# Diagonal sums on VectorE and GpSimd, y from the state on row tiles, and a compact state, from unit 8 on

## The chip, the cores and the metric

The kernel runs on one core of a Trainium2 chip. The core has five engines with queues of their own: TensorE (PE in the profile, with its weight loads apart as PEld), VectorE (DVE), ScalarE (ACT), GpSimd (POOL) and SyncE (SP, which here issues DMAs only). The metric is the device time of one execution in microseconds (us). The kernel before takes 174.02 us, the median of three runs (173.86 to 175.29).

## The reference

The reference has two stages. The first is a linear recurrence for 4 batches and 8 heads over 768 steps, with 48 x 48 states. The second is a two-layer feed-forward stage with a squared ReLU on the 3072 rows that come out of it.

```python
for t in range(S):
    cur = np.einsum('bhd,bhe->bhde', u[None] * kt, vt)
    y[:, :, t] = np.einsum('bhd,bhde->bhe', rt, state + cur)
    state = w[None, :, :, None] * state + np.einsum('bhd,bhe->bhde', kt, vt)
...
x = y.transpose(0, 2, 1, 3).reshape(B * S, H * D)      # 3072 x 384
h = x @ w_in                                           # 384 -> 2048
out = np.maximum(h, 0.0) ** 2 @ w_out                  # 2048 -> 384
```

What matters here is that y of one step has three parts: what earlier steps of the same chunk give (q k^T with a mask, times v), what the state at the chunk's start gives, and the diagonal: the step's own v, weighted for each head by the sum over d of r * k * u. The last one is the "diagonal sum".

## The kernel before

The 768 steps are cut into 6 chunks of 128, and a chunk of one batch is a **unit**. There are 24 of them, numbered chunk by chunk, so units 4c to 4c + 3 are the batches of chunk c. The name of a step carries its unit: `mask:9:1` is the second mask of unit 9. A unit has the token (time step) on the partitions after its load; a transposed copy has head and d on them.

For each unit the steps are these (line numbers of the kernel before):

- `load` brings r, k and v; `scale` (L288, DVE) multiplies r and k by powers of w into the tile rkw, padded from 48 to 64 per head; `cast_v` (L292, ACT) makes v bf16 as vb; `turn` or `turn_dma` (L302) transposes rkw into rkT, through PE or through a DMA.
- `rk` (L320, DVE) multiplies the transposed r and k into the tile rk. `sums` (PE) makes the diagonal sums from rk with four matmuls against a matrix uwb of u / w (L348, 8 columns each), and four more for the chunk's state update (L353).
- `at` (L328, PE) makes q k^T on row tiles: a head pair's two heads lie on the upper and the lower 64 partitions, so eight matmuls of 64 rows write two banks. `ats` does two units at once, from unit 8 on. `mask` (L340, DVE) takes each bank through the strict triangle into the tile am.
- `y_mm` (PE) adds up y in one bank: eight matmuls of am with vb (L391), and from chunk 1 on four matmuls of rkT with the state stb (L397). stb has two heads side by side in a block-diagonal tile of 96 columns, zero off the blocks.
- `diag_v` (L362, DVE) multiplies vb by the diagonal sums into dv; `evict_y` (L406, DVE) adds dv and y into yb; `x_dma` or `x_turn` transposes it into xT for the second stage.
- `state_add` (L372) and `state_decay` (L376), both on DVE, bring the float32 state forward; `state_cast` (L382, ACT) writes stb in two copies, one for each half of the partitions.

In the second stage, `mm1` (L435, PE) makes four blocks of h for one unit in the first two chunks, and eight blocks for two units from unit 8 on; `relu` (L443, ACT) and `square` (L454 on DVE or L452 on ACT, by the last number of its name) make g; `mm2` (L461, PE) multiplies by w_out in quarters, `evict_o` (L468, ACT) copies out, and `store` (L495) is issued by POOL. `fill` (L233) is a matmul of 256 columns on a constant tile whose result nobody reads.

The order is written out: the string SCHEDULE lists all steps, each engine runs its own in that order, and the number behind an @ names the PSUM banks (eight in all) that a step takes. A step waits until its inputs are there and its bank or buffer is free, and everything behind it on its engine waits too.

## Time and profile before

| | |
|---|---|
| median of three runs | 174.02 us |
| the profiled execution, its own time | 173.05 us |
| its span on the core | 171.3 us |
| granted TensorE clock, mean | 0.99 |
| HBM read and written | 20.45 MB, 4.72 MB |

The span is the time from the first to the last instruction that the profile records; the execution's own time has 1.75 us more around it. Shares of busy time are of the span. In rows of groups the number before the bar counts the instructions, then come their busy time in us, the mean of one in ns, the idle time of the engine just before them, and what ended that. A timeline row starts with its start and duration in us. Durations of consecutive matmuls overlap, since they are pipelined; differences of starts tell what one costs in a stream. For DVE two neighbours overlap by some 0.08 us.

### The profile page before, as it was taken

To read this page: it belongs to the slowest core of one execution; us is meant where nothing else is said; L and a number is where in the kernel's file an instruction comes from. 1 tells how busy PE (TensorE), PEld (TensorE's weight loads), DVE (VectorE), ACT (ScalarE), POOL (GpSimd) and SP (SyncE) were. 2 spreads that over 40 slices of the span, in tenths; PEclk is the share of its full clock that TensorE was granted. 3 is DMA by queue.
4 is the path that set the end of the run, shared out by engine and by line. 5 is a ranking of instruction groups with operands and counts; after the bars stand their busy time and mean duration, and the time that the engine had idled before them with its cause. 6 is when DMAs were issued, how large, how long until landed. Compare 5 with 4: busy or idle time off the path is not lost.

```text
span 171.3 us, 4810 instructions
## 1 busy us (share of the span) xinstructions
PE 164.8 (96%) x1931; PEld 132.1 (77%) x1931; DVE 138.0 (81%) x298; ACT 120.8 (71%) x252; POOL 30.5 (18%) x62
## 2 busy tenths in 40 slices
PE   7949999999999999999999999999999999999993
PEld 3637998787887788697796896896898776999662
DVE  5457997879999999999989879988989797764800
ACT  4533669999699547788599599499359986295830
POOL 8989440000002200000300000303000030030010
PEclk9987999999999999999999999999999999999999
DMA  5999999989996999899999999999959994150014
GB/s 106 199 212 213 220 249 244 222 157 158 187 169 120 286 145 169 166 186 148 238 229 123 182 186 128 254 149 204 262 97 211 201 150 134 32 161 0 4 62 168
DMA packets 94784, 28.83 MB, mean 168 GB/s; under 512 B 90665, under 2 KB 92714, under 8 KB 94762
## 3 DMA queue, kind: packets, MB, share of 16 engines
q1 hardware_dynamic: 90512, 19.08, 71.8%
q0 software_dynamic: 4224, 9.44, 21.1%
q8 instruction: 15, 0.25, 0.6%
q14 instruction: 7, 0.06, 0.1%
q10 hardware_dynamic: 26, 0.00, 0.0%
HBM read 20.45 MB, written 4.72 MB: 147 GB/s over the span
## 4 chain that ended last, share of the span: by engine, by line
PE 87%; DVE 5%; DMA 4%; POOL 2%; issue 1%; POOLq 0%; DVEq 0%
PE bank L461 35%; PE bank L435 35%; DMA ldr<-in_r_dram 4%; PE bank L328 4%; PE bank L391 3%; PE bank L353 2%; PE bank L397 2%; PE bank L476 2%; PE bank L233 1%; PE bank L311 1%; PE bank L348 1%; DVE yb L406 1%; DVE am L340 1%; DVE st L370 1%; PE bank L421 1%
## 5 line engine op out<-in xcount | busy, mean ns | idle before, releaser
L443 ACT ACTIVATE gr<-bank 128x512 f32<-128x512 f32 x96 | 53.8, 603 | 27.8 <-PE bank L435 24.4
L435 PE MATMUL bank<-xT,w_in_q 128*128 128x128 bf16 (+1 forms) x768 | 70.6, 246 | 0.0
L461 PE MATMUL bank<-w_out_q,g 128*128 128x384 bf16 x368 | 67.6, 326 | 0.0
L435 PEld LDWEIGHTS <-w_in_q 128*128 128x128 bf16 x768 | 64.1, 113 | 2.4
L461 PEld LDWEIGHTS <-g 128*128 128x128 bf16 x368 | 34.0, 98 | 18.9 <-ACT g L452 0.5
L454 DVE TENSOR_TENSOR g<-gr 128x512 bf16<-128x512 f32 x50 | 33.0, 686 | 6.5 <-ACT gr L443 6.4
L495 POOL DMA_DIRECT2D out_dram<-osb x21 | 11.3, 543 | 130.3 <-ACT osb L468 119.6
L340 DVE TENSOR_TENSOR am<-bank,smask 128x512 bf16<-128x512 f32 x48 | 30.8, 684 | 3.5 <-PE bank L328 3.2
L452 ACT ACTIVATE g<-gr 128x512 bf16<-128x512 f32 x46 | 28.2, 633 | 0.5
L406 DVE TENSOR_TENSOR yb<-bank,dv 128x384 bf16<-128x384 f32 x24 | 13.3, 556 | 3.9 <-PE bank L391 1.2
L288 DVE TENSOR_TENSOR rkw<-ldr,wpos 128x384 bf16<-128x384 f32 x24 | 12.9, 552 | 3.8 <-ACT wpos L241 2.2
L382 ACT CAST stb<-st 64x192 bf16<-64x192 f32 x40 | 13.9, 348 | 2.2 <-DVE st L376 1.9
L362 DVE TENSOR_TENSOR dv<-vb,bank 128x384 f32<-128x384 bf16 x24 | 13.0, 549 | 2.9 <-PE bank L353 2.1
L288 DVE TENSOR_TENSOR rkw<-ldk,wneg 128x384 bf16<-128x384 f32 x24 | 13.1, 552 | 0.6 <-DMA ldk<-in_k_dram 0.5
L292 ACT CAST vb<-ldv 128x384 bf16<-128x384 f32 x24 | 12.2, 512 | 0.6 <-DMA ldv<-in_v_dram 0.4
L468 ACT COPY osb<-bank 128x384 f32<-128x384 f32 x23 | 10.6, 481 | 2.7 <-PE bank L461 2.7
L372 DVE TENSOR_TENSOR st<-bank,st 64x192 f32<-64x192 f32 x32 | 11.3, 352 | 1.3 <-PE bank L353 1.0
L320 DVE TENSOR_TENSOR rk<-rkT 128x512 bf16<-128x512 bf16 x24 | 10.1, 419 | 1.9 <-ACT rkT L315 1.4
L233 PE MATMUL bank<-warm 128*128 128x256 bf16 x53 | 10.0, 336 | 1.2 <-DVE warm L179 1.2
L315 ACT COPY rkT<-bank 128x512 bf16<-128x512 bf16 x12 | 6.6, 591 | 4.1 <-PE bank L311 4.0
L328 PEld LDWEIGHTS <-rkT 64*128 64x128 bf16 x192 | 5.6, 95 | 4.6 <-issue 4.4
L328 PE MATMUL bank<-rkT 64*128 64x128 bf16 x192 | 8.1, 220 | 0.8 <-ACT rkT L315 0.8
(58 smaller groups left out, 112.6 us busy)
## 6 DMA issues: line engine op xcount, KB each, us to landing
ldk<-in_k_dram SPq DMA_DIRECT2D x22, 192.0 KB, 4.3
out_dram<-osb POOLq DMA_DIRECT2D x21, 192.0 KB, 3.5
ldr<-in_r_dram SPq DMA_DIRECT2D x20, 192.0 KB, 4.3
ldv<-in_v_dram SPq DMA_DIRECT2D x19, 192.0 KB, 4.5
w_in_q<-in_moe_w_in_dram POOLq DMA_DIRECT2D x4, 384.0 KB, 9.6
w_out_q<-in_moe_w_out_dram POOLq DMA_DIRECT2D x4, 384.0 KB, 10.8
ldv<-in_v_dram POOLq DMA_DIRECT2D x5, 192.0 KB, 9.6
ldr<-in_r_dram POOLq DMA_DIRECT2D x4, 192.0 KB, 8.9
```

The costliest lines, as they stand in the source:

```text
L288: nc.vector.tensor_tensor(t["rkw"][:, x, :, :, :D], pair(src), pair(wx), ALU.mult)
L292: nc.scalar.copy(tiles[i]["vb"], tiles[i]["vt"])
L328: nc.tensor.matmul(out=t["at"][o][:, p, :], lhsT=t["rkT"][sl, 1, p, :], rhs=t["rkT"][sl, 0, p, :], start=True, stop=True,)
L340: nc.vector.tensor_tensor(am, t["at"][o], smask.unsqueeze(1).to_broadcast([C, HP, C]), ALU.mult)
L362: nc.vector.tensor_tensor(t["dv"], t["vb"], t["d"].unsqueeze(2).to_broadcast([C, H, D]), ALU.mult)
L382: nc.scalar.copy(stb[b][sl, :, o * D : (o + 1) * D], st32[b][sl])
L406: nc.vector.tensor_tensor(t["yb"], t["y"], t["dv"].rearrange("p h d -> p (h d)"), ALU.add)
L435: nc.tensor.matmul(out=t["h", s][:, a], lhsT=turned, rhs=chunks[c]["xT"][:, n, b : b + m, :], start=(n == 0), stop=(n == NK - 1),)
L443: nc.scalar.activation(t["gr", s], t["h", s], AF.Relu)
L452: nc.scalar.activation(g, x, AF.Square)
L454: nc.vector.tensor_tensor(g, x, x, ALU.mult)
L461: nc.tensor.matmul(out=t["o"], lhsT=chunks[units[i][0]]["g"][:, f, units[i][1], :], rhs=w_out_q[f // 4][:, f % 4, :], start=(f == 0), stop ...
```

## The change

From unit 8 on (chunk 2 and later) three things are done in another way, and the order of all steps is written anew:

- **Diagonal sums.** `rk` and the four L348 matmuls go. In token layout, `product` (DVE) multiplies scaled r and k of the 384 real columns into pr; `weigh` (POOL) multiplies by u / w, which two broadcast loads (`wide_load`) and one product (`wide_product`) put on all partitions once; two `fold` steps (POOL) add halves of each head, 48 to 24 to 12; `head_sums` (DVE) reduces the last 12. `diag_v` reads the sums from SBUF instead of PSUM.
- **y.** The state's part is made by eight matmuls of 64 rows and 48 columns a unit, right behind q k^T of both units inside `ats`, in two banks (even heads and odd heads) that hold both units. `ys` adds the mask's part of both units. `evict_y` reads two half tiles.
- **State.** The bf16 state stc keeps one head's 48 columns on each half of the partitions, with no zeros, so `state_cast` is one copy; this begins with the casts of unit 4, which unit 8 reads.

`ats` thus takes six banks where it took four. Of 96 squares, DVE has 30 where it had 50, and ACT 66 where it had 46. Of fills there are 34 where there were 53.

```diff
+    WIDE_FROM = 8
...
+    stc = [const.tile([128, HP, D], BF16, name=f"stc_{b}") for b in range(B)]
+    wide = [const.tile([128, H, D], F32, name=f"wide{x}") for x in range(2)]
...
+    def wide_load(x):
+        src = (w, u)[x].rearrange("h d -> (h d)").unsqueeze(0).to_broadcast([128, dm])
+        nc.sync.dma_start(out=wide[x].rearrange("p h d -> p (h d)"), in_=src)
+    def wide_product():
+        nc.gpsimd.tensor_tensor(wide[1], wide[1], wide[0], ALU.mult)
+    def product(i):
+        t = tiles[i]
+        t["pr"] = buffer("pr", [C, H, D], BF16)
+        nc.vector.tensor_tensor(pair(t["pr"]), t["rkw"][:, 0, :, :, :D], t["rkw"][:, 1, :, :, :D], ALU.mult)
+    def weigh(i):
+        t = tiles[i]
+        t["pw"] = buffer("pw", [C, H, D], F32)
+        nc.gpsimd.tensor_tensor(t["pw"], t["pr"], wide[1], ALU.mult)
+    def fold(i, n):
+        x = tiles[i]["pw"]
+        m = D >> (n + 1)
+        nc.gpsimd.tensor_tensor(x[:, :, :m], x[:, :, :m], x[:, :, m : 2 * m], ALU.add)
+    def head_sums(i):
+        t = tiles[i]
+        t["d"] = buffer("ds", [C, H], F32)
+        nc.vector.tensor_reduce(out=t["d"], in_=t["pw"][:, :, : D // 4], axis=mybir.AxisListType.X, op=ALU.add)
...
     def ats(i):
         at(i)
         at(i + 1)
+        for j in (i, i + 1):
+            y = halves(j)
+            for p in range(HP):
+                for o in range(2):
+                    sl = slice(o * 64, o * 64 + 64)
+                    nc.tensor.matmul(
+                        out=y[o][:, p, :], lhsT=tiles[j]["rkT"][sl, 0, p, :], rhs=stc[units[j][1]][sl, p, :],
+                        start=(j == i and p == 0), stop=False, skip_group_check=True,
+                    )
...
-        for p in range(HP):
+        for p in range(HP if i < WIDE_FROM else 0):
             nc.tensor.matmul(
                 out=t["d"], lhsT=t["rk"][:, p, :], rhs=uwb[:, p, :],
...
+        if i >= WIDE_FROM - B:
+            nc.scalar.copy(stc[b], st32[b])
+        for o in range(2 if i < WIDE_FROM - B else 0):
...
+    def ys(i):
+        for j in (i, i + 1):
+            t = tiles[j]
+            y = halves(j)
+            for p in range(HP):
+                for o in range(2):
+                    nc.tensor.matmul(
+                        out=y[o][:, p, :], lhsT=t[f"am{o}"][:, p, :], rhs=t["vb"][:, 2 * p + o, :],
+                        start=False, stop=j > i and p == HP - 1, skip_group_check=True,
+                    )
...
+        if i >= WIDE_FROM:
+            out_y = t["yb"].rearrange("c (a o d) -> c o a d", o=2, d=D)
+            dv = t["dv"].rearrange("c (a o) d -> c o a d", o=2)
+            for o, y in enumerate(halves(i)):
+                nc.vector.tensor_tensor(out_y[:, o], y, dv[:, o], ALU.add)
+            return
```

The schedule's first line, before and after:

```diff
-load:1:kt:SP fill:256@7 load:0:rt:SP 2*fill:256@7 load:0:kt:SP 2*fill:256@7 load:1:rt:POOL 2*fill:256@7 load:2:kt:SP
+load:0:rt:SP load:1:kt:SP load:0:kt:SP load:1:rt:POOL load:2:kt:SP columns:1 columns:0 load:2:rt:POOL spread_log@0
```

Three places show what moves. On PE before, `sums` of unit 16 has the four diagonal matmuls (rk, uwb) ahead of those for the state (vb, rkw):

```order
L348 LDWEIGHTS rk_2134
L348 MATMUL bank7_68<-uwb_145,rk_2134 128x8
L348 LDWEIGHTS rk_2134
L348 MATMUL bank7_68<-uwb_145,rk_2134 128x8
L348 LDWEIGHTS rk_2134
L348 MATMUL bank7_68<-uwb_145,rk_2134 128x8
L348 LDWEIGHTS rk_2134
L348 MATMUL bank7_68<-uwb_145,rk_2134 128x8
L353 LDWEIGHTS rkw4_121
L353 MATMUL bank7_68<-vb_2152,rkw4_121 128x96
```

On PE after, the end of q k^T of units 16 and 17 (L363) is followed by the state's part of y of unit 16 (L379), whose halves go to banks 3 and 7:

```order
L363 LDWEIGHTS rkT_2027
L363 MATMUL bank4_65<-rkT_2027 128x128
L363 LDWEIGHTS rkT_2027
L363 MATMUL bank2_63<-rkT_2027 128x128
L379 LDWEIGHTS rkT_2089
L379 MATMUL bank3_64<-stc_0_160,rkT_2089 128x48
L379 LDWEIGHTS rkT_2089
L379 MATMUL bank7_68<-stc_0_160,rkT_2089 128x48
L379 LDWEIGHTS rkT_2089
L379 MATMUL bank3_64<-stc_0_160,rkT_2089 128x48
```

The diagonal matmuls are gone from PE, and the state's part of y has moved ahead of the masks, onto the row tiles.

On DVE before, around the masks of units 16 and 17 (am), stand the two rk products and the decays of the state (st32):

```order
L320 TENSOR_TENSOR rk_2134<-rkT_1964 128x512
L340 TENSOR_TENSOR am1_2160<-bank4_65,smask_140 128x512
L376 TENSOR_TENSOR st32_2_149<-st32_2_149,wend_c_159 128x192
L320 TENSOR_TENSOR rk_2170<-rkT_1995 128x512
L340 TENSOR_TENSOR am0_2178<-bank7_68,smask_140 128x512
L340 TENSOR_TENSOR am1_2182<-bank5_66,smask_140 128x512
L288 TENSOR_TENSOR rkw0_117<-ldr0_97,wpos_94 128x8x48
L340 TENSOR_TENSOR am0_2199<-bank0_61,smask_140 128x512
L362 TENSOR_TENSOR dv_2215<-vb_2152,bank7_68 128x384
```

On DVE after, from the second product of that pair (pr) to the first reduction (ds), with the state sums (L420), scales (L296), a square (L521) and the masks (L387) between:

```order
L335 TENSOR_TENSOR pr_2129<-rkw5_122 128x384
L420 TENSOR_TENSOR st32_3_150<-bank1_62,st32_3_150 64x192 x2
L296 TENSOR_TENSOR rkw0_117<-ldk2_105,wneg_95 128x8x48
L420 TENSOR_TENSOR st32_2_149<-bank2_63,st32_2_149 64x192 x2
L296 TENSOR_TENSOR rkw1_118<-ldr1_98,wpos_94 128x8x48
L521 TENSOR_TENSOR g_2085<-gr_2170 128x2x256
L387 TENSOR_TENSOR am1_2228<-bank2_63,smask_140 128x512
L387 TENSOR_TENSOR am0_2236<-bank1_62,smask_140 128x512
L387 TENSOR_TENSOR am1_2246<-bank0_61,smask_140 128x512
L387 TENSOR_TENSOR am0_2250<-bank4_65,smask_140 128x512
L296 TENSOR_TENSOR rkw0_117<-ldr0_97,wpos_94 128x8x48
L350 TENSOR_REDUCE ds_2269<-pw_2133 128x8
```

The products have left the neighbourhood of the masks and stand well ahead, and the reduction stands behind the masks, where diag_v read PSUM before.

On POOL, which had only stores behind its loads, the same pair has these rows after (L340 is `weigh`, L345 `fold`, DMA a store):

```order
L340 TENSOR_TENSOR pw_2133<-pr_2119,wide1_165 128x384
L345 TENSOR_TENSOR pw_2133<-pw_2133 128x8x24
L340 TENSOR_TENSOR pw_2168<-pr_2129,wide1_165 128x384
L345 TENSOR_TENSOR pw_2168<-pw_2168 128x8x24
L562 DMA out_0_dram<-osb_1931 128x384
L345 TENSOR_TENSOR pw_2168<-pw_2168 128x8x12
L562 DMA out_0_dram<-osb_2177 128x384
L562 DMA out_0_dram<-osb_1914 128x384
L345 TENSOR_TENSOR pw_2133<-pw_2133 128x8x12
```

Stores of finished rows now stand between the folds.

207 lines of the change are left out of this document (107 added, 100 removed).

## The prediction

> **What bounds the kernel now.** I read the page's shares first, then the busy slices, then the chain that ended last.
>
> ```profile
> span 171.3 us, 4810 instructions
> ...
> PE 164.8 (96%) x1931; PEld 132.1 (77%) x1931; DVE 138.0 (81%) x298; ACT 120.8 (71%) x252; POOL 30.5 (18%) x62
> ...
> PE   7949999999999999999999999999999999999993
> ...
> PE 87%; DVE 5%; DMA 4%; POOL 2%; issue 1%; POOLq 0%; DVEq 0%
> ```
>
> TensorE (PE) is busy in every slice from the fifth on, and 87% of the chain is its own instructions one behind the other. A busy PE alone could hide waiting, but the chain names almost no releaser after the first 25 us, so there PE's queue is the time. VectorE (DVE) at 81% is second. I cut the steady part into stretches from one q k^T group to the next; this is units 16 and 17, with busy time of PE, weight loads, DVE, ACT and POOL:
>
> ```profile
> 106.54:118.92 12.38, 12.38 (x139) 9.99 (x141) 10.64 (x23) 9.97 (x23) 1.99 (x4) 1.00 1.04 194
> ```
>
> A pair of units costs 12.38 us of PE, and DVE idles 1.74 us of it, ACT 2.4 us. A change is therefore worth what it takes from PE, as long as DVE's work, with its waits, stays below PE's.
>
> **The change on PE.** The timeline gives what the small matmuls cost inside the stream, as differences of starts (the durations overlap):
>
> ```profile
> 87.74 0.36 PE L391 MATMUL bank<-vb,am 128*128 128x48 bf16 x8
> ...
> 87.94 0.33 PE L397 MATMUL bank<-stb,rkT 128*128 128x96 bf16 x4
> ...
> 88.11 0.24 PE L348 MATMUL bank<-uwb,rk 128*128 128x8 bf16 x4
> ...
> 88.21 0.33 PE L353 MATMUL bank<-vb,rkw 128*128 128x96 bf16 x4
> ...
> 94.09 0.62 PE L328 MATMUL bank<-rkT 64*128 64x128 bf16 x16
> ...
> 94.64 1.47 PE L461 MATMUL bank<-w_out_q,g 128*128 128x384 bf16 x8
> ```
>
> - Diagonal sums: four matmuls of 8 columns stand from 88.11 to 88.21, 0.10 us. Sixteen units lose them: 16 x 0.10 = **-1.6 us**.
> - y from the state: four matmuls of 96 columns take 88.11 - 87.94 = 0.17 us. In their place come eight of 48 columns on 64 rows. No row shows that form. The row for 48 columns on all rows gives 8 x 0.025 = 0.20 us; the q k^T row, the only one on row tiles, gives 0.55 / 16 = 0.034 each, 0.27 us; if two tiles ran wholly side by side at the 48-column pace it would be 0.10 us. I take 0.20, whose column count is the same: 16 x (0.20 - 0.17) = **+0.5 us**, with -1.1 and +1.6 as ends.
> - y from the mask keeps its eight matmuls a unit, and the switch between row tiles and full rows still happens once per q k^T group: nothing.
> - Fill matmuls: 53 become 34, but ten of them now stand behind the point where PE is saturated (two more are at the very end, behind the last real matmul). One of 256 columns costs what the 256-column group shows:
>
> ```profile
> 34.42 0.67 PE bank L435 x12
> ...
> 148.21 4.58 PE bank L435 x42
> ```
>
> 4.58 / 42 = 0.109 us, so **+1.1 us** where PE would have had work, and nothing where it would have waited. I take the whole.
>
> Steady part: -1.6 + 0.5 + 1.1 = 0.0 us.
>
> **The start.** The order is rewritten from the first word. Rows of the first 25 us:
>
> ```profile
> 4.17 0.88 POOL L267 DMA_DIRECT2D ldr<-in_r_dram  x1
> ...
> 11.75 0.55 DVE L288 TENSOR_TENSOR rkw<-ldk,wneg 128x384 bf16<-128x384 f32 x1
> ...
> 12.23 2.48 DVE L340 TENSOR_TENSOR am<-bank,smask 128x512 bf16<-128x512 f32 x4
> ...
> 15.02 1.05 PE L233 MATMUL bank<-warm 128*128 128x256 bf16 x8
> ...
> 16.36 0.56 DVE L406 TENSOR_TENSOR yb<-bank,dv 128x384 bf16<-128x384 f32 x1 [1.20 <-PE bank L391]
> ...
> 20.78 1.15 PE L233 MATMUL bank<-warm 128*128 128x256 bf16 x9
> ...
> 23.27 0.56 DVE L406 TENSOR_TENSOR yb<-bank,dv 128x384 bf16<-128x384 f32 x1
> ```
>
> Before, all four masks of units 0 and 1 come first, eight fills stand ahead of unit 1's y, the third y leaves DVE at 23.83, and PE bridges with nine fills. After, DVE does two masks, unit 1's y, and the three y's with no state sum between them: behind the scale that ends at 12.3 stand six masks at 2.48 / 4 = 0.62, three diagonal products, one rk product and three evictions (0.55, 0.42 and 0.56, from the groups L362, L320 and L406 below), 7.5 us, so the third y is out near 19.8, 4.0 us sooner. Unit 2's r load is also one POOL issue (0.9 us) earlier. Not all of it is time: ACT is nearly full there. I count the nine-fill bridge, 1.0 us, and half of the eight-fill one, 0.5: **-1.5 us**. The ends are -3 (most of the 4.0) and +1.5, since fewer fills may leave the clock low for longer; it is already 0.83 (third value from the right) in this stretch:
>
> ```profile
> 10.00:20.00 10.00, 8.40 (x113) 6.93 (x113) 7.41 (x16) 3.25 (x7) 7.11 (x17) 0.83 1.20 220
> ```
>
> **What moves to the other engines, and what hides it.**
>
> ```profile
> L454 DVE TENSOR_TENSOR g<-gr 128x512 bf16<-128x512 f32 x50 | 33.0, 686 | 6.5 <-ACT gr L443 6.4
> L495 POOL DMA_DIRECT2D out_dram<-osb x21 | 11.3, 543 | 130.3 <-ACT osb L468 119.6
> L340 DVE TENSOR_TENSOR am<-bank,smask 128x512 bf16<-128x512 f32 x48 | 30.8, 684 | 3.5 <-PE bank L328 3.2
> L452 ACT ACTIVATE g<-gr 128x512 bf16<-128x512 f32 x46 | 28.2, 633 | 0.5
> L406 DVE TENSOR_TENSOR yb<-bank,dv 128x384 bf16<-128x384 f32 x24 | 13.3, 556 | 3.9 <-PE bank L391 1.2
> ...
> L382 ACT CAST stb<-st 64x192 bf16<-64x192 f32 x40 | 13.9, 348 | 2.2 <-DVE st L376 1.9
> L362 DVE TENSOR_TENSOR dv<-vb,bank 128x384 f32<-128x384 bf16 x24 | 13.0, 549 | 2.9 <-PE bank L353 2.1
> ...
> L372 DVE TENSOR_TENSOR st<-bank,st 64x192 f32<-64x192 f32 x32 | 11.3, 352 | 1.3 <-PE bank L353 1.0
> L320 DVE TENSOR_TENSOR rk<-rkT 128x512 bf16<-128x512 bf16 x24 | 10.1, 419 | 1.9 <-ACT rkT L315 1.4
> ```
>
> DVE, per unit: the 512-element product (0.42) becomes one of 384 (between 0.35, the 192-element row, and 0.42; I take 0.35); the eviction of y becomes two of 192 (2 x 0.352 - 0.556 = +0.15); the new reduction reads 96 elements, which no row shows: at most the 0.352 of 192, at least nothing beside its neighbours; I take 0.25. Together +0.33 a unit, 0.67 a pair. Against that, 20 of DVE's 50 squares go to ACT, 11 of them between the first and the last paired q k^T: 11 / 7 x 0.686 = 1.1 a pair. DVE goes from 10.64 to about 10.2 of about 12.2 us, leaving 2.0 us. ACT gains 20 x 0.633 and loses 16 casts of 0.348 (one compact copy in place of two): 120.8 + 7.1 = 127.9 us, 75%. Neither becomes the bound by its own work. The compact cast must now be done before the q k^T group, not before y; DVE's idle time covers that.
>
> POOL gets three instructions a unit, of 384, 192 and 96 elements; its 21 stores (0.54 us each, L495) stand between them, and each waits for its eviction on ACT, so a fold behind a store waits too, and with it the reduction on DVE and all that is queued behind that. The nearest rows have one input:
>
> ```profile
> masks.py:66 POOL TENSOR_SCALAR_AFFINE_SELECT smask<-smask 128x128 f32<-128x128 f32 x1 | 0.3, 293 | 0.1
> ...
> masks.py:199 POOL TENSOR_SCALAR_AFFINE_SELECT ident<-ident 4x4 f32<-4x4 f32 x1 | 0.2, 184 | 0.1
> ```
>
> (293 - 184) / 124 = 0.88 ns an element; from a 0.2 us base that is 0.53 + 0.36 + 0.28 = 1.2 us a unit, and with two inputs read in turn twice the slope, 0.87 + 0.53 + 0.36 = 1.8 us. I take 1.8, since both operations have two inputs: 3.5 us a pair, inside 12 us. The Trainium skill, GPSIMD Engine Reference, section 3.1, gives 4497 ns for such an operation on 2048 elements; by it a unit would cost an estimated 2.1 us and a pair 4.1, and the sum would stay as it is. Two added broadcast loads and two extra SP issues before unit 8 are hidden by loads that run far ahead.
>
> **What speaks against it.** POOL and DVE do not run freely beside each other:
>
> ```profile
> 11.28 0.56 DVE L288 TENSOR_TENSOR rkw<-ldr,wpos 128x384 bf16<-128x384 f32 x1 [1.45 <-DMA ldr<-in_r_dram]
> 11.37 0.52 POOL L260 TENSOR_TENSOR wend_c<-wend_c 128x4 f32<-128x4 f32 x1
> ...
> L260 POOL TENSOR_TENSOR wend_c<-wend_c x6: 198/198/522, 11.1 to 13.0; 128x4 f32<-128x4 f32 x6
> ```
>
> Six equal POOL instructions take 198 ns, but the one that starts 0.09 us behind a DVE product of two SBUF tiles takes 522 and ends at 11.89, just behind DVE's 11.84. POOL waited for DVE. Whether DVE waits as long behind a POOL instruction the rows cannot show, since POOL's were tiny. If it does, scales, squares, decays, products and diagonal products are exposed; masks, evictions and state sums, which read PSUM, are not. In order, the weigh instructions mostly meet state sums and masks, so I expect about 1 us of such waits a pair, inside the 2.0 us.
>
> The Trainium skill, SBUF — State Buffer, section "Who interferes with whom", says that a DVE instruction with two SBUF inputs and a GpSimd one that reads SBUF exclude each other for a whole instruction, whoever is first. The trace agrees for POOL's side (522 against 198 ns); by that rule DVE waits as well, which is the first rival.
>
> **The sum.** 0.0 - 1.5 = -1.5 us. The profiled execution took 173.05 us; the median of the runs is 174.02, and I carry the difference over to it: 174.0 - 1.5 = **172.5 us**. A measurement of this kernel tells about 1%, 1.7 us, from no change.
>
> **The rivals.**
> - *DVE waits for POOL* (slower). If DVE loses a microsecond for most of POOL's 3.5, say 2.7 a pair, its 10.2 becomes 12.9 against 12.2, and PE waits 0.7 us in each of eight pairs: 172.5 + 5.6 = 178.1 us. It decides from 2.0 us of waits a pair. For it: a POOL instruction outlasts a DVE one, and half of DVE's time is of the exposed kind. Against it: the order above.
> - *POOL's sums come late* (slower). From the first product of a pair to the second reduction POOL has 3.5 us, two stores of 0.54 and perhaps 2 us of blocking, 6.6; DVE's own work between them in units 16 and 17 is four state halves, three scales, a square and four masks, 6.5. One more microsecond a pair in DVE, y and the next input tiles: 172.5 + 8 = 180.5 us.
> - *A cold start*: the start loses what it should win, +1.5 for -1.5: 175.5 us.
> - *Row tiles pair fully* (faster): 0.10 us for 0.20, 16 x 0.10 = 1.6: 170.9 us. The q k^T row speaks for some of it: 0.55 / 8 = 0.069 a pair of 128 columns, where one of 128 columns on all rows takes 0.67 / 12 = 0.056 (the row at 34.42). The Trainium skill, TensorE: Matmul & The Clock Gate, Part 3, states that row tiles run concurrently with about 4 ns between starts; this row agrees in part, and by that rule this rival would be the result.
>
> **How the numbers follow.** The forecast has 0.48, split evenly about -1%, since 172.5 lies there; DVE waiting for POOL 0.24, late sums 0.10, a cold start 0.10, paired tiles 0.08. Faster by over 1%: 0.24 + 0.08 = 0.32. Within 1%: 0.24 + 0.10 = 0.34. Slower: 0.34. The range reaches from 169.8 (the start's better end or paired tiles) to 178.5 (past the first rival); late sums and the outer ends are left out.
>
> **What would show it.** PE busy nearly without gaps from 20 us on, the first paired q k^T near 58, the L379 group at 0.20 us per unit; DVE's scale and square groups still near 552 and 686 ns at the median. Wrong would be: those groups' maxima near 1.2 us, PE waiting for DVE at the am or y tiles, POOL's weigh far over 0.9 us, or a clock under 0.8 up to 24 us.

## The result, and the profile after

The changed kernel takes **182.7 us** (median of 4 runs, 179.7 to 184.4), the kernel before 174.1. Every ratio here and below is to the kernel before, with a 95% interval, and leaves out executions that took over 1.5% longer than the fastest of the same kernel, so here it compares 179.7 and 181.6 us with 174.1: **1.038** (1.031 to 1.045). Forecast were 172.5 us and a range of 169.8 to 178.5. The profiled execution took 179.74 us, against 173.05 before; the page of the changed kernel, with the rows that answer to those shown of before:

```profile
span 178.0 us, 4856 instructions
...
PE 162.1 (91%) x1912; PEld 129.1 (73%) x1912; DVE 133.8 (75%) x310; ACT 123.6 (69%) x256; POOL 65.0 (37%) x111
...
PE   2958897999999969989699999989999999999992
...
PEclk9996599999999999999999999999999999999999
...
PE 59%; DMA 24%; DVE 5%; ACT 4%; SPq 4%; issue 2%; DVEq 0%
```

The stretch of units 16 and 17, again from one q k^T group to the next (length, then busy time of PE, PEld, DVE, ACT and POOL, then granted clock, DMA share, GB/s):

```profile
112.45:124.85 12.40, 11.83 (x134) 9.54 (x135) 11.30 (x27) 8.39 (x19) 3.37 (x6) 1.00 0.90 188
```

It is as long as before, 12.4 us, with half a microsecond of TensorE idle in it.

TensorE is 2.7 us *less* busy than before, VectorE 4.2, and yet the span is 6.7 us longer. The chain says where to look: TensorE's own instructions were 87% of it and are 59%; transfers were 4% and are 24%. The longest piece of that chain is one load (start, length, what):

```profile
6.62 23.05 DMA ldk<-in_k_dram
29.68 0.02 issue
29.70 0.56 DVE rkw L296
30.26 0.34 DVE rk L355
...
31.37 0.38 PE bank L319 x4
```

It is the k of unit 5: issued at 6.62 us, landed at 29.7. VectorE's queue holds the scaling of that k (L296) *ahead* of unit 3's product r k^T (L355), so unit 3 waits for unit 5. Unit 3's own input, the transposed tile rkT, had been ready at 28.3 us, when ScalarE's copy ended:

```profile
27.75 0.59 ACT L323 COPY rkT<-bank 128x512 bf16<-128x512 bf16 x1
```

TensorE's timeline shows this wait and the others of over 1 us behind the first 10 us (idle time and its releaser in brackets):

```profile
13.31 0.33 PE L401 MATMUL bank<-vb,rkw 128*128 128x96 bf16 x4 [1.22 <-ACT vb L300]
...
30.65 0.26 PE L396 MATMUL bank<-uwb,rk 128*128 128x8 bf16 x4 [1.07 <-DVE rk L355]
...
88.08 0.40 PE L363 MATMUL bank<-rkT 64*128 64x128 bf16 x8 [1.72 <-DMA rkT<-rkw]
```

The wait at 13.31 is of the same kind, with ScalarE as the engine whose queue is held up. Its timeline in the changed kernel, and behind it in the kernel before:

```profile
12.34 0.92 ACT L300 CAST vb<-ldv 128x384 bf16<-128x384 f32 x2 [2.49 <-DMA ldv<-in_v_dram]
```

```profile
9.32 0.51 ACT L292 CAST vb<-ldv 128x384 bf16<-128x384 f32 x1
...
21.26 0.54 ACT L292 CAST vb<-ldv 128x384 bf16<-128x384 f32 x1
```

Before, unit 1's v is cast at 9.32 us without a wait and unit 2's only at 21.26. The new order puts unit 2's cast first; it waits 2.49 us for its load, and unit 1's cast and the first state sums wait behind it.

The new operations themselves did nothing of the sort. These are the groups of GpSimd's three instructions and, on VectorE, of the squares, the product and the reduction (count, busy time, mean ns, idle time before them):

```profile
L340 POOL TENSOR_TENSOR pw<-pr,wide 128x384 f32<-128x384 bf16 x16 | 17.0, 1069 | 50.6 <-DVE pr L335 50.5
L345 POOL TENSOR_TENSOR pw<-pw 128x192 f32<-128x192 f32 x16 | 10.3, 645 | 0.7
L345 POOL TENSOR_TENSOR pw<-pw 128x96 f32<-128x96 f32 x16 | 7.0, 444 | 0.6
```

```profile
L521 DVE TENSOR_TENSOR g<-gr 128x512 bf16<-128x512 f32 x30 | 22.5, 762 | 6.8 <-ACT gr L510 6.5
...
L335 DVE TENSOR_TENSOR pr<-rkw 128x384 bf16<-128x384 bf16 x16 | 6.0, 395 | 0.1
...
L350 DVE TENSOR_REDUCE ds<-pw 128x8 f32<-128x96 f32 x16 | 3.6, 244 | 0.5 <-POOL pw L345 0.3
```

GpSimd takes 2.16 us a unit and waits 50 us for VectorE's products; VectorE's reduction waited 0.3 us for GpSimd in the whole run. The squares are stretched (762 ns for 686), as the first rival said, but VectorE is idle for a quarter of the span.

That gives **theory T**: the time went to the new order, which asks at the start for loads that land late, in queues that then hold up work that is ready. Against it stand **R1** (GpSimd holds VectorE), **R2** (GpSimd's sums are late) and **R3** (fewer fills, a cold clock). The R1, R2, R3 and T of the expectations below are these.

### The profile page after: what moved, and what is told of

The parts are those of the page before. It is cut to its first block, busy times and chain, and to the rows that moved or that the text cites. A ratio compares the mean times of both kernels' runs of the same rounds, so it can differ in the third digit from the quotient of the medians.

```text
span 178.0 us, 4856 instructions
## 1 busy us (share of the span) xinstructions
PE 162.1 (91%) x1912; PEld 129.1 (73%) x1912; DVE 133.8 (75%) x310; ACT 123.6 (69%) x256; POOL 65.0 (37%) x111
## 4 chain that ended last, share of the span: by engine, by line
PE 59%; DMA 24%; DVE 5%; ACT 4%; SPq 4%; issue 2%; DVEq 0%
PE bank L502 25%; PE bank L528 25%; DMA ldk<-in_k_dram 13%; DMA ldv<-in_v_dram 5%; SPq L275 4%; DMA xT<-yb 3%; DMA rkT<-rkw 3%; PE bank L363 2%; ACT gr L510 2%; PE bank L440 2%; PE bank L543 1%; DVE am L387 1%; ACT g L519 1%; PE bank L401 1%; DVE st L420 1%
## 5 line engine op out<-in xcount | busy, mean ns | idle before, releaser
L510 ACT ACTIVATE gr<-bank 128x512 f32<-128x512 f32 x96 | 55.1, 602 | 30.6 <-PE bank L502 30.2
L502 PE MATMUL bank<-xT,w_in_q 128*128 128x128 bf16 (+1 forms) x768 | 72.9, 249 | 1.5 <-ACT xT L492 0.6
L502 PEld LDWEIGHTS <-w_in_q 128*128 128x128 bf16 x768 | 65.7, 115 | 5.6 <-issue 1.6
L519 ACT ACTIVATE g<-gr 128x512 bf16<-128x512 f32 x66 | 39.8, 633 | 0.4
L340 POOL TENSOR_TENSOR pw<-pr,wide 128x384 f32<-128x384 bf16 x16 | 17.0, 1069 | 50.6 <-DVE pr L335 50.5
L387 DVE TENSOR_TENSOR am<-bank,smask 128x512 bf16<-128x512 f32 x48 | 30.9, 685 | 4.9 <-PE bank L363 3.8
L521 DVE TENSOR_TENSOR g<-gr 128x512 bf16<-128x512 f32 x30 | 22.5, 762 | 6.8 <-ACT gr L510 6.5
L296 DVE TENSOR_TENSOR rkw<-ldk,wneg 128x384 bf16<-128x384 f32 x24 | 14.1, 588 | 7.5 <-DMA ldk<-in_k_dram 5.3
L345 POOL TENSOR_TENSOR pw<-pw 128x192 f32<-128x192 f32 (+1 forms) x32 | 17.1, 545 | 1.3
L296 DVE TENSOR_TENSOR rkw<-ldr,wpos 128x384 bf16<-128x384 f32 x24 | 13.2, 552 | 1.8 <-DMA ldr<-in_r_dram 1.6
L420 DVE TENSOR_TENSOR st<-bank,st 64x192 f32<-64x192 f32 x32 | 11.3, 354 | 1.2 <-PE bank L401 0.7
L471 DVE TENSOR_TENSOR yb<-bank,dv 128x192 bf16<-128x192 f32 x32 | 9.8, 352 | 1.2 <-PE bank L440 0.7
L363 PE MATMUL bank<-rkT 64*128 64x128 bf16 x192 | 8.0, 218 | 2.2 <-DMA rkT<-rkw 2.0
L363 PEld LDWEIGHTS <-rkT 64*128 64x128 bf16 x192 | 5.5, 94 | 5.8 <-DMA rkT<-rkw 2.9
L410 DVE TENSOR_TENSOR dv<-vb,ds 128x384 f32<-128x384 bf16 x16 | 8.9, 560 | 1.0 <-ACT vb L300 0.7
```

What stands on the lines that cost most here:

```text
L296: nc.vector.tensor_tensor(t["rkw"][:, x, :, :, :D], pair(src), pair(wx), ALU.mult)
L340: nc.gpsimd.tensor_tensor(t["pw"], t["pr"], wide[1], ALU.mult)
L345: nc.gpsimd.tensor_tensor(x[:, :, :m], x[:, :, :m], x[:, :, m : 2 * m], ALU.add)
L363: nc.tensor.matmul(out=t["at"][o][:, p, :], lhsT=t["rkT"][sl, 1, p, :], rhs=t["rkT"][sl, 0, p, :], start=True, stop=True,)
L387: nc.vector.tensor_tensor(am, t["at"][o], smask.unsqueeze(1).to_broadcast([C, HP, C]), ALU.mult)
L420: nc.vector.tensor_tensor(st32[b][sl], x, st32[b][sl], ALU.add)
```

## The experiments

The lines of the schedule are steps in program order; in the diffs a step that is not named stays where it is, and "..." stands for steps left out.

### Is it GpSimd? Its work taken away, and the load's place changed

**e1_no_pool**: the changed kernel without weighting and folds.

```diff
- weigh:i  fold:i:0  fold:i:1
- nc.vector.tensor_reduce(out=t["d"], in_=t["pw"][:, :, : D // 4], ...)
+ nc.vector.tensor_reduce(out=t["d"], in_=t["pr"][:, :, : D // 4], ...)
```

> The changed kernel with the weighting and both folds on GpSimd left out; the reduction reads the unweighted product instead (so u, w and three quarters of the products are left out of the diagonal sums). GpSimd then computes nothing in the loop and cannot hold VectorE or be late. Theory T (the time went to transfers that the new order needs before they land): the waits on ldk, ldv, rkT and xT stay, at most VectorE's 4 to 4.5 us of stretched operations spread over a quarter-idle engine go, so 0 to 1 us less than the changed kernel (ratio to the kernel before 1.03 to 1.045). Rival R1 (VectorE held by GpSimd) or R2 (sums late): the 5 to 8 us go, ratio 0.99 to 1.005.

Measured: 1.046 (1.037 to 1.055). No gain, although the squares fell to 686 ns: R1 and R2, which asked for 0.99 to 1.005, are out for this order.

**e2_unit5_later**: unit 5's scalings behind unit 4's, its turns and q k^T with them.

```diff
  wout:3:0
- scale:5:0  ...  scale:5:1  ...  rk:3 at:3
+ rk:3 at:3
  ...
  evict_y:3  ...  scale:4:0
+ scale:5:1 scale:5:0
```

> The changed kernel with unit 5's two scalings, its two turns and its q k^T moved behind unit 4's, so that nothing ahead of unit 4 needs unit 5's k, which landed at 29.67 us. Theory T: TensorE's wait of 1.07 + 0.27 us for the product of unit 3 goes, 1.3 to 2.5 us less than the changed kernel (ratio to the kernel before 1.024 to 1.035), and the first paired q k^T starts 1 to 2 us sooner than at 61.8 us. Rival R3 (the clock and the fills at the start): nothing moves, ratio 1.038. R1 and R2: nothing moves either.

Measured: 1.026 (1.020 to 1.033), as T has it, though the interval still touches that of the changed kernel. The first paired q k^T did not come sooner in the profiled execution, the longest of its four (62.6 us, against 61.8 in the changed kernel); the other wait was longer there (TensorE's timeline):

```profile
15.01 0.48 PE L401 MATMUL bank<-vb,rkw 128*128 128x96 bf16 x4 [2.96 <-ACT vb L300]
```

### The second wait of the start

**e5_cast_order**: as e2_unit5_later, and ScalarE's casts exchanged.

```diff
- cast_v:2 fill@2 rk:1 ... at:1@0,3 cast_v:1 ... evict_rk:2:0
+ cast_v:1 fill@2 rk:1 ... at:1@0,3 ... evict_rk:2:0 cast_v:2
```

> The kernel with unit 5 later, and besides it ScalarE's cast of unit 1's v ahead of that of unit 2 (the changed kernel has unit 2's first, and the kernel before casts it 12 us later); in the changed kernel unit 1's cast stood behind unit 2's, which waited 2.5 us for its v, 4.0 us in the profile with unit 5 later, and TensorE waited 1.2 and 3.0 us behind it. Theory T: those waits go, and with them part of the 0.71 granted clock between 10 and 20 us, 1.5 to 3 us less than with unit 5 later alone (ratio to the kernel before 1.008 to 1.018), and less scatter. Rival R3 (the fewer fills): the clock stays near 0.71 and the gain is 0 to 1 us.

Measured: **1.003** (0.999 to 1.007), 10 runs of 173.2 to 177.3 us: of the 3.8% that the change lost, two moves in two queues give back 3.5, some 6.1 us. The first mm1 stands at 17.88 us in the kernel before and at 15.49 here:

```profile
17.88 0.83 PE L435 MATMUL bank<-xT,w_in_q 128*128 128x128 bf16 x12
```

```profile
15.49 0.83 PE L502 MATMUL bank<-xT,w_in_q 128*128 128x128 bf16 x12
```

TensorE's clock between 10 and 20 us, in the kernel with unit 5 later and in this one (the clock is the third value from the right):

```profile
10.00:20.00 10.00, 7.04 (x95) 5.62 (x94) 7.03 (x14) 2.84 (x7) 6.86 (x18) 0.71 1.20 220
```

```profile
10.00:20.00 10.00, 8.39 (x148) 6.63 (x147) 9.11 (x18) 5.45 (x11) 6.86 (x17) 1.00 1.20 220
```

Both kernels have the same fills, so R3 as it was put (fewer fills keep the clock down) is out: without the 3 us gap the granted clock is 1.00 and 148 matmuls fit where 95 did. Nor is a low clock needed for the loss: one execution of the changed kernel, of 181.6 us, had a granted clock of 1.00 over its whole span.

**e7_cast_only**: the exchanged casts without the move of unit 5.

> The changed kernel with ScalarE's cast of unit 1's v ahead of that of unit 2, and nothing else; unit 5 stays where the change has it. Theory T (two waits at the start, one behind the other, each for a load that the new order asks for too soon): the cast's share is what it was with unit 5 later, 2.3% of the kernel before, so ratio 1.01 to 1.02, and unit 5's 1 to 2 us stay. If one wait only covered the other: 1.025 to 1.04.

Measured: 1.044 (1.038 to 1.051), a miss: alone, the exchange gains nothing. Rows of TensorE and of VectorE in the profiled execution, the longest of its four:

```profile
33.87 0.27 PE L396 MATMUL bank<-uwb,rk 128*128 128x8 bf16 x4 [6.09 <-DVE rk L355]
```

```profile
32.92 0.56 DVE L296 TENSOR_TENSOR rkw<-ldk,wneg 128x384 bf16<-128x384 f32 x1 [7.71 <-DMA ldk<-in_k_dram]
```

VectorE waited 7.71 us for that k, 5.0 more than in the changed kernel's profile (2.75): 3.2 of them because the k landed later in this execution (32.9 us instead of 29.7), 1.7 because VectorE came sooner. What the exchanged casts win is waited away there, and TensorE's clock was 0.66 between 30 and 40 us, against 1.00. So the waits do not add up: the one for unit 5's k hides what the other costs, and a faster start gained nothing until it was gone.

### The same two steps in the kernel before

```diff
  cast_v:1 ... relu:1:1:2
+ scale:5:0 scale:5:1
  rk:3 at:3
```

**f1_before_unit5** has this; **f2_before_both** also has `cast_v:2` ahead of `cast_v:1`.

> The kernel before with one thing of the new order put in: VectorE's two scalings of unit 5 stand ahead of unit 3's r k^T product (at 25.75 us in the trace of before) instead of at 29 and 37 us. None of the change's operations is in it. Theory T: VectorE waits there for unit 5's k, which landed at 29.67 to 32.9 us in the traces of the changed order, the product of unit 3 comes at 31 to 34 us where TensorE asked for it at 29.9, 1.5 to 4.5 us more and a dip of the granted clock behind it, ratio 1.01 to 1.035. If the wait only hurts in company with the change's operations: 0.997 to 1.005.

> The kernel before with both things of the new order put in: unit 5's scalings ahead of unit 3's product, and ScalarE's cast of unit 2's v ahead of that of unit 1. Theory T: the cast waits for its v until 12 to 14 us and delays the first sums by 1 to 3 us, but the k of unit 5 lands when it lands, so most of it is covered by the later wait, ratio 1.015 to 1.04, of which the changed kernel's 1.038 to 1.044 would be made whole. If the start of the changed kernel costs otherwise: below 1.01.

Measured: 1.015 (1.008 to 1.021) and 1.012 (1.006 to 1.017). Without one operation of the change the same wait appears; in the profiled execution of the first, the longest of its four (175.4 to 182.0 us), VectorE and TensorE show

```profile
34.12 0.56 DVE L289 TENSOR_TENSOR rkw<-ldk,wneg 128x384 bf16<-128x384 f32 x1 [8.49 <-DMA ldk<-in_k_dram]
```

```profile
35.80 0.25 PE L349 MATMUL bank<-uwb,rk 128*128 128x8 bf16 x4 [6.19 <-DVE am L341]
```

The k landed at 34.1 us there, at 28.5 in the profile of f2_before_both and at 29.7 in that of the changed kernel: the landing scatters from one kernel's profile to the next. But the second expectation was missed: both steps together cost the kernel before 1.2%, not the 3.5% that they cost the changed one. A difference between the two kernels fits: with the waits gone, the changed order has its first mm1 at 15.49 us, the kernel before at 17.88, so a wait that ends at the landing eats 2.4 us more there. The scatter of the landing fits too: the four executions of f1_before_unit5 lie between 175.4 and 182.0 us, and the profile of f2_before_both had the earliest landing of all. Both are argued from the rows, not tried.

### Can the loads be had sooner?

**f4_k5_sooner**: unit 5 where the change has it, casts exchanged, and the load of unit 5's k ahead of unit 2's v and unit 5's r.

```diff
- load:2:kt:SP ... load:2:vt:SP ... load:5:rt:SP ... load:5:kt:SP
+ load:2:kt:SP ... load:5:kt:SP load:2:vt:SP ... load:5:rt:SP
```

> The changed kernel with the cast of unit 1's v first, unit 5 where the change has it, and the load of unit 5's k two places sooner on SyncE's queue, ahead of unit 2's v and unit 5's r. The cast alone gave nothing (1.044, VectorE then waited 7.7 us for that k and TensorE 6.1). Theory T: with the k there in time (landing some us sooner than 29.7 to 32.9) the wait goes without a step of VectorE moved, ratio 1.00 to 1.015, unless unit 2's v now comes late by as much. If the k lands no sooner, because the channels are full and not the queue: 1.03 to 1.045.

Measured: 1.044 (1.039 to 1.049). The wait for k is gone; in its place ScalarE and TensorE show

```profile
20.11 0.93 ACT L300 CAST vb<-ldv 128x384 bf16<-128x384 f32 x2 [7.36 <-DMA ldv<-in_v_dram]
```

```profile
20.67 0.48 PE L401 MATMUL bank<-vb,rkw 128*128 128x96 bf16 x4 [7.06 <-ACT vb L300]
```

I read this as the transfers being the limit there: 220 GB/s at a DMA share of 1.20 between 10 and 20 us in the two rows above and in that of the kernel before, and 218 to 221 GB/s in all profiles here, whatever the order. The load that went ahead made another late.

The same was tried four times with the later loads. **e3_v_early** issues the v loads from unit 11 on sooner, in the changed kernel; **e4_rk_loads** those of r and k from unit 13 on, with unit 5 later; **e8_three_loads** only r and k of 13 and k of 15, with both corrections; **f3_both_and_queue** puts three loads behind two turns instead and one scaling behind two masks.

```diff
# e3
- turn_dma:10 turn_dma:11 load:11:vt:SP ... load:12:vt:SP
+ load:11:vt:SP ... load:12:vt:SP load:13:vt:SP turn_dma:10 turn_dma:11
# e4 (units 16 and 17)
- load:17:kt:SP turn_dma:14 load:19:kt:SP load:17:rt:SP ... load:16:rt:SP ... load:16:kt:SP
+ load:16:rt:SP load:16:kt:SP load:17:rt:SP load:17:kt:SP turn_dma:14
# e8
- x_dma:9 x_dma:8 load:13:rt:SP load:13:kt:SP
+ load:13:rt:SP load:13:kt:SP x_dma:9 x_dma:8
# f3
- load:13:vt:SP load:14:rt:SP load:14:kt:SP turn_dma:12 turn_dma:13
+ turn_dma:12 turn_dma:13 load:13:vt:SP load:14:rt:SP load:14:kt:SP
```

> The changed kernel with its v loads from unit 11 on issued some steps sooner on SyncE's queue, ahead of the turning transfers behind which they stood; nothing else moves. Theory T: ScalarE's waits for ldv (6.3 us in five places) and what follows on TensorE (0.57 us of bank wait at 117.87, 1.2 us for vb) go, 1 to 3 us less than the changed kernel (ratio to the kernel before 1.02 to 1.033). R1, R2, R3: no difference, ratio 1.038. If the transfers as a whole are the limit, waits move from ldv to the turned tiles and the time stays within 0.5 us.

> The kernel with unit 5 later, and besides it the loads of r and k from unit 13 on issued one group sooner on SyncE's queue, ahead of the two turning transfers of the pair before instead of behind them and behind the two of y. In the changed kernel r of unit 13 was issued at 76.15 us, behind 4.8 us of y's transfers, its scaling waited 1.08 and 0.48 us for r and k, its turn landed at 88.03 and TensorE waited 1.72 us. Theory T (transfers asked for late and needed early): that wait goes, 1.5 to 3 us less than with unit 5 later alone (ratio to the kernel before 1.008 to 1.018). If the transfers as a whole are the limit: other waits take its place, as for v alone, ratio 1.025 to 1.05.

> The kernel with both corrections of the start, and three loads a step sooner on SyncE's queue: r and k of unit 13 ahead of y's two transfers of units 9 and 8 (not ahead of the turns of units 10 and 11), and k of unit 15 ahead of those of units 10 and 11. In the profile with both corrections TensorE waited 1.12 us for a turn at 83.14 and VectorE 2.37 us for a k at 87.47. Theory T: 0.5 to 1.2 us less, ratio to the kernel before 0.995 to 1.001. If y's transfers come late instead: 1.003 to 1.02.

> The kernel with both corrections of the start, and two small moves in the steady part: VectorE's scaling of unit 10's k behind unit 9's masks (TensorE waited 0.38 and 0.61 us there, at 59.8 and 61.2), and the loads of v of unit 13 and of r and k of unit 14 behind the turns of units 12 and 13 on SyncE's queue (TensorE waited 1.12 us for the second). Theory T: 0.5 to 1.5 us less than with both corrections alone, ratio to the kernel before 0.994 to 1.001. If other transfers come late in their place, as with the three loads: 1.003 to 1.012.

Measured, in that order: 1.050 (1.040 to 1.060), 1.074 (1.068 to 1.079), 1.007 (1.004 to 1.011) and 1.026 (1.019 to 1.032): no gain in any, so what T expected was missed four times; only e8_three_loads came out as the other branch of its expectation had it. Each profile has new or longer waits. In e3_v_early TensorE waits 3.8 us for turned tiles (2.0 in the changed kernel) and 2.5 for y's (0.5). In e4_rk_loads k of unit 17, which VectorE takes before r of unit 16, had come to stand last of four loads (VectorE); in e8_three_loads TensorE waits, ahead of a weight load, for y's transfer, now two loads later; in f3_both_and_queue, whose profiled execution is one of its longer ones (179.9 us of 176.7 to 180.1), VectorE waits for r of unit 14:

```profile
104.14 0.56 DVE L296 TENSOR_TENSOR rkw<-ldk,wneg 128x384 bf16<-128x384 f32 x1 [4.87 <-DMA ldk<-in_k_dram]
```

```profile
74.49 2.55 PEld L502 LDWEIGHTS <-w_in_q 128*128 128x128 bf16 x24 [1.99 <-DMA xT<-yb]
```

```profile
86.15 0.56 DVE L296 TENSOR_TENSOR rkw<-ldr,wpos 128x384 bf16<-128x384 f32 x1 [4.53 <-DMA ldr<-in_r_dram]
```

So in none of these could a transfer be had sooner without making another one late.

**e9_no_late_fills** leaves the seven single fills behind the first paired q k^T out of e8_three_loads; **e10_order_no_pool** is e5_cast_order without GpSimd's work; **g1_first_pair** is e5_cast_order with the broadcasts of u and w, GpSimd's u*w and unit 9's product sooner, for the two waits at the first pair (0.38 us at 59.77, 0.61 at 61.19).

```diff
# e9
- mm2:5:3 fill@6 mm2:7:0@1
+ mm2:5:3 mm2:7:0@1
# e10
- weigh:i  fold:i:0  fold:i:1
# g1
- turn_dma:7 wide_load:1 ... wide_load:0 ... product:9 product:8
+ wide_load:1 wide_load:0 ... turn_dma:7 wide_product ... product:9 weigh:9 ... product:8
```

> The same with the seven single fills behind the first paired q k^T left out of TensorE. If they stand on the path (the prediction has fills at 0.11 us each): 0.7 us less than with them, ratio 0.991 to 0.997. If TensorE would have waited there anyway: no difference.

> The kernel with both corrections of the start and with the weighting and both folds on GpSimd left out (u, w and three quarters of the products are left out of the diagonal sums). With the waits of the start gone, GpSimd's share shows alone. Theory T: within 0.6 us of the kernel with both corrections, ratio 0.998 to 1.007. Rival R1 or R2: 1.5 us or more goes, ratio below 0.995.

> The kernel with both corrections of the start, and the first pair's diagonal sums begun sooner: the two broadcast loads of u and w on SyncE's queue behind r of unit 9, GpSimd's u*w behind unit 7's turn, and unit 9's product and weighting ahead of unit 8's scaling. With the corrections alone VectorE's two products of units 9 and 8 took 1.38 us at 54.4 and the next square 1.43 (0.69 alone), beside GpSimd's first products, and TensorE waited 0.38 and 0.61 us behind them. If that stretch is what is left of GpSimd's hold on VectorE: 0.5 to 1 us less, ratio to the kernel before 0.995 to 1.001. If not: 1.001 to 1.01.

Measured: 1.011 (1.007 to 1.015), 1.010 (1.005 to 1.016), 1.014 (1.009 to 1.018). No cost of the fills shows: without them TensorE's one large wait, for y's transfer near 74.9 us, is 2.81 us long where it was 1.63. GpSimd's work costs nothing in this order, once more. And g1_first_pair removed its two waits and got a larger one, for the turn of unit 7, which now stands behind the broadcasts:

```profile
54.50 0.40 PE L363 MATMUL bank<-rkT 64*128 64x128 bf16 x8 [2.84 <-DMA rkT<-rkw]
```

### The change in the order of the kernel before

**a2_all_old_order** has the whole change there: products right behind the scalings, head sums where r k^T stood, the state part of y right ahead of the pair's first y. (PSUM banks are given out anew where it needs more of them, and one mm1 result of units 10 and 11 and one of units 16 and 17 are overwritten before they are read; the work is all there.) **a2b_squares** shares the squares as the changed kernel does, and has the two relus of those results one step sooner. **a1_sums_only** has the diagonal sums alone, **a4_sums_no_pool** the same without GpSimd's work.

```diff
  scale:i:0 ... scale:i:1
+ product:i weigh:i fold:i:0 fold:i:1
  ...
- rk:i
+ head_sums:i
# a2, a2b
- y_mm:i ... y_mm:i+1
+ yst:i ysj:i ... ysj:i+1
# a2b, twenty squares more on ScalarE
- square:5:1:0:0
+ square:5:1:0:1
# a4
- weigh:i fold:i:0 fold:i:1
```

> The whole change (diagonal sums on VectorE and GpSimd, compact state, y from the state as row tiles of two banks a pair) in the order of the kernel before: each product right behind its scaling, the head sums where r k stood, the state part of y right ahead of the pair's first y, squares shared as before. Theory T: the new operations cost TensorE 2.7 us less than before and hide on the other engines, so ratio 0.98 to 1.00 (170.6 to 174). R1 and R2 (the operations themselves cost the time, by the lock or by late sums): 1.02 to 1.045, whatever the order. VectorE has 11.3 us of work in a pair of 12.2 us here, so up to 1.01 would still fit T.

> The whole change in the order of the kernel before, with the squares shared as in the changed kernel (66 on ScalarE, 30 on VectorE) instead of 46 and 50. VectorE was 98% busy between 60 and 90 us without this. Theory S: VectorE falls to about 10.5 us in a pair and the waits of TensorE for g, yb and st (4.6 us) go, ratio 0.985 to 1.01 against 1.045. Rival R1 (GpSimd's hold on VectorE costs time wherever it stands): 1.02 to 1.04.

> The diagonal sums alone (product on VectorE, weighting and folds on GpSimd, reduction on VectorE) in the order of the kernel before, y and state as before, squares shared as before. TensorE loses 1.6 us of work. VectorE has 10.64 + 0.5 us a pair, and 0.7 more if GpSimd holds it as often as in the kernel with the whole change in the old order (g 754 instead of 686 ns, decay 443 instead of 352), that is 11.8 of 12.3. Theory S (in the old order VectorE's share, and not the transfers, costs the time): ratio 1.00 to 1.02. If the sums are harmless: 0.985 to 0.995.

> The diagonal sums alone in the order of the kernel before, with the weighting and both folds on GpSimd left out (u, w and three quarters of the products are left out of the sums); product and reduction stay on VectorE. With them VectorE was busy 150.1 us against 138.0, of which product and reduction in place of the old product make 2.8, so some 9 us would be operations stretched beside GpSimd (squares 768 instead of 686 ns, diagonal products 631 instead of 549, decays 444 instead of 352). If GpSimd's hold is what cost 4.7% in that order: VectorE falls to about 141 us and the ratio to 0.99 to 1.015. If the place of the steps cost it: above 1.03.

Measured: 1.045 (1.039 to 1.051), 1.038 (1.032 to 1.044), 1.047 (1.042 to 1.052), **1.005** (1.001 to 1.008). The first three were missed: I had the operations free of cost in any order, and they are not. The last shows why. VectorE's groups in a1_sums_only and behind them in a4_sums_no_pool:

```profile
L524 DVE TENSOR_TENSOR g<-gr 128x512 bf16<-128x512 f32 x50 | 37.1, 768 | 6.1 <-ACT gr L513 5.9
L391 DVE TENSOR_TENSOR am<-bank,smask 128x512 bf16<-128x512 f32 x48 | 30.8, 684 | 2.2 <-PE bank L365 1.6 <-ACT g L522 0.4
...
L414 DVE TENSOR_TENSOR dv<-vb,ds 128x384 f32<-128x384 bf16 x16 | 9.9, 631 | 0.0
L428 DVE TENSOR_TENSOR st<-st,wend_c 128x192 f32<-128x192 f32 x16 | 7.1, 444 | 0.1
```

```profile
L521 DVE TENSOR_TENSOR g<-gr 128x512 bf16<-128x512 f32 x50 | 33.0, 686 | 6.7 <-ACT gr L510 6.5
L388 DVE TENSOR_TENSOR am<-bank,smask 128x512 bf16<-128x512 f32 x48 | 30.9, 684 | 2.7 <-PE bank L362 2.3
...
L411 DVE TENSOR_TENSOR dv<-vb,ds 128x384 f32<-128x384 bf16 x16 | 8.6, 550 | 0.0
...
L425 DVE TENSOR_TENSOR st<-st,wend_c 128x192 f32<-128x192 f32 x16 | 5.6, 352 | 0.1
```

With GpSimd at work VectorE's squares, diagonal products and decays, which read SBUF alone, are longer, and its masks, which read PSUM, are not (684 ns in both). In all it is busy 150.1 us against 140.8; for GpSimd's sums themselves it waited nowhere. And here VectorE has no slack. Between 60 and 90 us, with and without GpSimd's work:

```profile
60.00:90.00 30.00, 28.13 (x332) 21.63 (x330) 29.48 (x62) 20.53 (x43) 12.13 (x18) 1.00 0.97 177
```

```profile
60.00:90.00 30.00, 29.69 (x357) 23.85 (x350) 29.05 (x65) 21.88 (x47) 1.60 (x3) 1.00 1.06 188
```

VectorE is as full in both, but with GpSimd's work it does 62 instructions instead of 65, and TensorE 332 matmuls instead of 357. So R1 is real: 9.3 us of VectorE and 4.2% of the time where VectorE has nothing to spare, and no time in the order of the changed kernel, where it is idle for 25% of the span. Idle time is not shown to be the whole condition: in a2b_squares VectorE was idle for 24% and the ratio stayed at 1.038. Its profile has a 2.09 us wait of TensorE for the state sums at 117.31, with operations of up to 0.94 us in front of it, but no kernel without GpSimd's work was run beside it. So what the whole change costs in the order of the kernel before, with the squares moved, stays open.

## Why the prediction was wrong

Point by point, in the order of the prediction:

- **What bounds the kernel** held for the kernel before, and the condition put to it (as long as VectorE's work, with its waits, stays below TensorE's) is what a1_sums_only and a4_sums_no_pool measured. It left out that TensorE can also wait for a transfer.
- **The change on PE.** The diagonal sums' 0.10 us a unit stands. The state part of y was taken at 0.20 us a unit and measures half, in the changed kernel's chain:

```profile
88.47 0.20 PE bank L379 x16
...
93.36 0.40 PE bank L440 x16
```

  Sixteen matmuls on row tiles, two units, take 0.20 us, sixteen on all rows 0.40. So this term was -1.1 us, not +0.5: the cost that the rival of fully paired tiles had, 0.10 us a unit. The Trainium skill, TensorE: Matmul & The Clock Gate, Part 3, states that row tiles run concurrently. The row agrees (12.5 ns a matmul against 25); the 4 ns between two starts no row here shows. The fills' +1.1 did not show: without seven of them e9_no_late_fills was no faster (1.011 against 1.007).
- **The start: this is the step that failed.** The -1.5 us were counted from VectorE's instructions up to the third y as if every input were there. Up to there most of the gain came: the third y left VectorE at 21.0 us, against 19.8 forecast and 23.8 before, and at 18.1 with both waits gone.

```profile
20.47 0.56 DVE L473 TENSOR_TENSOR yb<-bank,dv 128x384 bf16<-128x384 f32 x1 [1.40 <-PE bank L452]
```

  What the working left at nothing is the wait for loads: the new order moves unit 5's scalings ahead of unit 3's product and unit 2's cast ahead of unit 1's, and nothing asked when those loads land. In place of -1.5 us the start lost some 6.1, which e5_cast_order gave back (1.038 to 1.003). The trace of before had the answer. SyncE issues unit 5's k at 6.64 us there, and its landing is the slowest of all loads of k, 26.2 us later, at 32.8:

```profile
6.64 3.60 SPq L267 DMA_DIRECT2D ldk<-in_k_dram  x1
```

```profile
DMA to landing us min/median/max: 3.2/4.7/26.2
```

  The last sentence on the other engines, that the extra issues are "hidden by loads that run far ahead", is the same mistake; the loads of the start do not run ahead. And even with both waits gone the gain did not last: the first mm1 starts 2.4 us sooner than before (15.49 against 17.88), the first paired q k^T only 0.1 (58.52 against 58.63).
- **What moves to the other engines** was sized nearly right. The reduction took 0.244 us (0.25 taken), GpSimd 2.16 us a unit (1.8 taken), and ScalarE is busy 123.6 us (127.9 worked out). The estimate of 2.1 us that was worked out from a figure of the Trainium skill, GPSIMD Engine Reference, section 3.1, was nearer than the 1.8. VectorE's stretch was put at 1 us a pair inside 2.0 us of slack; in the changed kernel the squares alone make 30 x 0.076 = 2.3 us in the run.
- **The rivals.** DVE waiting for POOL did not decide this kernel (e1_no_pool, e10_order_no_pool), and does decide a1_sums_only, with the same sums and no slack: 9.3 us in eight pairs is 1.2 a pair, where VectorE had 12.38 - 10.64 = 1.7 us less 0.35 for the added work of product and reduction. The Trainium skill, SBUF — State Buffer, section "Who interferes with whom", states that either side can be the one that waits. The longer squares, diagonal products and decays of a1_sums_only agree for VectorE's side, which the trace of before could not show. Late sums: 0.3 us in the run. A cold start went the right way, at +1.5 us where +6 came, and by another cause: the waits came first, and the same fills without them had a clock of 1.00.
- **What would show it**: of the signs of a right forecast, TensorE without gaps from 20 us on and the first paired q k^T near 58 did not come (61.8); the medians of scales and squares did (552 and 688 ns). Of the signs of a wrong one, the clock under 0.8 came (0.74 between 10 and 20 us), and so did single long squares (up to 1.76 us). The long squares pointed at GpSimd, which e1_no_pool then cleared.
- **The range.** Its lower end of 169.8 follows from neither term it names (the start's better end gives 171.0, paired tiles 170.9). Nothing here hangs on it.

**Where the gain went that is left.** With both waits gone the time is that of before, not 1.5 us less. The page of e5_cast_order, and the first 10 us of the kernel before and of it:

```profile
span 171.9 us, 4857 instructions
...
PE 160.4 (93%) x1912; PEld 127.3 (74%) x1912; DVE 133.7 (78%) x310; ACT 123.9 (72%) x256; POOL 65.0 (38%) x111
```

```profile
0.00:10.00 10.00, 8.01 (x54) 5.11 (x55) 5.45 (x29) 5.42 (x9) 9.21 (x21) 1.00 0.94 158
```

```profile
0.00:10.00 10.00, 6.57 (x33) 4.01 (x34) 5.24 (x29) 4.92 (x8) 9.21 (x21) 1.00 0.95 159
```

TensorE is busy 4.4 us less than before (164.8) and idle 5.0 us more. Of those, 1.4 are in the first 10 us, where fills were left out and nothing could stand in their place (one wait of 3.2 us for ScalarE's lnw, which the changed kernel has too); 0.95 lie between 30 and 40 us (0.85 of them a wait for a mask); 2.1 are three waits at the first pairs (0.38, 0.61 and 1.12 us); the rest, some 0.5, lies behind 160 us. The work was saved, but not on the path.

One thing stays open. From the first paired q k^T to the end the order of e5_cast_order is that of the changed kernel, yet it takes 113.4 us there (171.9 - 58.52) against 116.2 (178.0 - 61.82). So 2.8 of the 6.1 us between the two profiles lie behind the start, in an order that is the same. Which of the start's waits moves which later transfer was not found.

No kernel here beats the one before.

## What to carry to other kernels

Ask of every step that a new order moves forward in an engine's queue when its input lands, and which ready steps stand behind it; the trace of before holds the landing (here 26.2 us behind the issue). Waits for landings need not add up: one correction gave 1.026, the other 1.044, both 1.003, so remove all that stand in a row before judging any one of them. And where one engine's work makes another's longer, measure with the neighbour's work and without, in the order that will be used: here the same work cost nothing in one order and 4.2% in another.

## What I had not expected of the hardware

- One load of 192 KB at the start (unit 5's k) took 22.0 to 26.8 us from issue to landing (f2_before_both and f1_before_unit5; 26.2 in the kernel before), against a median of 4.7 for the loads of k over the whole run, and its landing moved by 5.6 us between profiles (28.5 to 34.1).
- Moving one load two places forward made another 6 to 8 us late (unit 2's v at 20.1 us instead of 12.3 to 14.2).
- With the fills of the new start, a wait of 1.0 to 7.1 us on TensorE that began between 10 and 20 us went with a granted clock of 0.71 to 0.85 over that stretch (six profiles, 0.74 in the changed kernel and 0.83 in e7_cast_only with waits of 1.2 us); with waits of at most 0.73 us it was 1.00 (seven profiles, e5_cast_order among them). The kernel before, with a wait of 1.6 us there, had 0.83.
- Of five rearrangements of loads and turning transfers on SyncE's queue none gained: three cost 1.0, 2.2 and 4.7% of the kernel before (g1_first_pair, f3_both_and_queue, e4_rk_loads), and two (e3_v_early, e8_three_loads) are not told from the kernel they start from, by their intervals.
